# PSUM banks as tiles of their own, and a seven-product first MoE matmul with Silu for the last two batches

## The chip, the cores and the metric

The kernel runs on one core of a Trainium2 chip. The metric is the device time of one execution in microseconds (us). A core has engines that work side by side: TensorE (PE; its weight loads are PEld), VectorE (DVE), ScalarE (ACT), GpSimd (POOL) and SyncE (SP), which issues transfers. Matmul results land in PSUM, which the kernel uses as eight banks of 128 partitions by 512 fp32 values.

## The reference

Softmax attention for 8 batches, 12 heads, 448 tokens, head size 64. Its output, heads side by side, is the input of a two-layer block with a SiLU between (called MoE in the kernel):

```python
scores = q @ k.T / sqrt(64);  attn = softmax(scores);  y = attn @ v
x = y.transpose(0, 2, 1, 3).reshape(8 * 448, 768)
h = x @ w_in                       # 3584 x 768  times 768 x 2048
g = h * (1.0 / (1.0 + exp(-h)))    # SiLU
out = g @ w_out                    # 3584 x 2048 times 2048 x 768
```

## The kernel before

All matmul inputs are fp16, sums are fp32. A planner in Python (`Order`) walks a model of the engines and fixes the order in which each engine gets its instructions; the program then adds the waits that the data and the buffers need, by tile. The kernel is one core's, and every buffer is allocated once. These are its parts that the change and the prediction touch; cuts are marked with `# ...`.

PSUM and its banks. Banks 0 to 3 are for attention scores, in two pairs (a pair takes two heads); banks 4 to 7 (`M`) are for everything else: attention outputs, first and second MoE matmul. `lent()` says which score banks the rest may use when scores don't need them.

```python
P_s = [ps.tile([128, 2, 512], FP32, name=f"p_{i}") for i in range(4)]

def bank(i):
    return P_s[i // 2][:, i % 2]
# ...
M = (4, 5, 6, 7)

def lent():
    if not qk_seq or silu_phase() or LEND and e_slots.when(1) is None:
        return 0, 1, 2, 3
    return ()

def m_take():
    more = lent()
    i = min((*M, *more), key=lambda i: (banks.free[i] > od.now, i < 4, banks.free[i]))
    # ...
```

Attention (L383 scores, L408 Exp, L432 sums of Exp and products with V, L454/L459 inverse sums by transposes, L465 scaling):

```python
def expo(n, w, y, s_pair, e_i):
    # ...
    nc.scalar.activation(out=E_s[e_i][0:kr, 2 * y : 2 * y + 2, 0:nk],
                         in_=P_s[s_pair][0:kr, :, 0:nk], func=AF.Exp, scale=attn_scale)
# attend(): nc.tensor.matmul(out=bank(a)[32 * h : 32 * (h + 1), 0:nq], ...)      L432
# inverse(): nc.vector.transpose(out=t, in_=grouped(n, bank(a)))                 L454
# norm():    x = bank(a) * 0.5 * t   on VectorE, to x_s (xT in the profile)      L465
```

The first MoE matmul, plain form (all eight batches before the change). One of 16 blocks `f` of the hidden layer takes six matmuls into one bank. x carries a factor 0.5, so SiLU is (tanh(x) + 1) * x: a Tanh on ScalarE, then a gate on VectorE that reads the bank and writes G (or X):

```python
def ffn1_plain(b, f, t0, t1, a, c0, c1):
    for cc in range(c0, c1):
        nc.tensor.matmul(out=bank(a)[:, 0 : t1 - t0],                            # L485
            lhsT=w_in_t[:, cc, 128 * f : 128 * (f + 1)],
            rhs=x_s[x_at[(b, cc // HC)]][:, cc % HC, t0:t1], start=(cc == 0), # ...
def tanh(src, th):
    nc.scalar.activation(out=th, in_=src, func=AF.Tanh)                          # L498
def gate(eng, out, th, x):
    (nc.vector if eng == "DVE" else nc.gpsimd).scalar_tensor_tensor(             # L501
        out=out, in0=th, scalar=1.0, in1=x, op0=ALU.add, op1=ALU.mult)
def silu(out, src):
    nc.scalar.activation(out=out, in_=src, func=AF.Silu, scale=2.0)
# class Plain.run(), after the sixth matmul:
    done = od.add(Op("ACT", act(t1 - t0), lambda: tanh(x, th), [op], ...))
    # then, for each part, gate("DVE", dst[:, f, ...], th, x) with deps [done]; its end frees the bank
```

The first MoE matmul, folded form (class `Fold`), which is in the kernel before but used by no batch there. A batch's tokens, the 768 inputs and the 2048 hidden values are each halved, and a block of two by two halves is made from seven products (Strassen's scheme in Winograd's form) where the plain form takes eight. Each product is three matmuls of 224 columns; eight folds (`HF`) make a batch. Products 1, 2 and 5, 6, 3 share a bank side by side, 7 and 4 take a second bank:

```python
class Fold:
    ORDER = (1, 5, 2, 6, 7, 3, 4)
    # deps of product 1: the x of the batch, t_op (four differences of x on VectorE),
    #   and all output items that still read the part of G that this batch overwrites
    def run(self):
        # ... three matmuls of S // 2 = 224 columns
        if m == 5:   # copy products 1 and 5 (448 columns) on ScalarE or VectorE
        elif m == 6: # y = A + p1 on VectorE;  p5 = y - p5 on GpSimd
        elif m == 3: # c12 = A + p1 on VectorE, in the bank;  finish(bank, f)
        elif m == 4: # c21 = p5 + B on VectorE;  finish(F, f + HF)
        # after 6 and 7: c22 = B + y on VectorE
    def finish(self, src, ff, deps, psum):
        if b < SILU:   # Tanh, then gate, as in the plain form
        # else: Silu on ScalarE from src straight to G
```

While a batch with Silu is under way (`silu_phase()`), no new scores are started. The differences of `w_in` that folds need (`SI`, and one written over a quarter of `w_in`) are made in the kernel before as well.

The second MoE matmul (class `Quad`, L804): pairs of 128 tokens, 14 items in all, each also seven products, of eight matmuls of 384 columns, given to TensorE two at a time (`CUT = 2`). It works in two banks, `w` (products 1, 2, 3) and `q` (5, 6, 7, 4). Between products VectorE adds (L510) and ScalarE copies (L514) out of a bank; its left-hand sums (S, sometimes kept in E buffers) are added by VectorE and GpSimd from G.

```python
self.ORDER = (1, 5, 2, 6, 7, 3, 4)
# ... in run(): op = Op("PE", (i1 - i0) * mm(n), lambda: self.emit(m, a, ...))
if m == 1:   ev["p1"] = od.add(Op("ANY", {...}, lambda e: copy(e, p, W), [op], SLOW))
elif m == 5: add("r", r, Q, p, [op, ev["p1"]])
elif m == 2: ev["c11"] = self.write(0, 0, W, self.w, [op], None)
elif m == 6: add("y", W, Q, r, [op, ev["c11"]])
elif m == 7: add("c22", r, Q, r, [op, ev["y"]])   # ... and its store
elif m == 3: self.write(0, 1, W, self.w, [op], ...)
else:        add("c21", p, Q, p, [op, ev["c22"]], ...)   # ... and its store
```

Of the kernel before, what the change touches and what calls it, by code (L numbers as in the profile page):

```python
# [8 lines left out]
FP32 = mybir.dt.float32  # L9
# [191 lines left out]
def kernel(  # L201
# [28 lines left out]
    NT = 2 * S // 128  # L230
    OH = DM // 2
    PACE = 2.3
    DEFER, DITEM = .3, .1
    SUMS, EKEEP, ESENG = (0, 1), 2, 'VP'
    QB = 4
    LIM_H = 3
    LIM_E, LIM_S, LEND = 2, 2, 1
    LONE = NG + 1
    PLAIN = 8
    SILU = 8  # L240
    HIGH = 'POOL'
    ZENG = 'POOL'
    PIECES = ((0, 7), (7, TPP))
# [7 lines left out]
    ps = ctx.enter_context(tc.tile_pool(name="ps", bufs=1, space=bass.MemoryType.PSUM))  # L251
# [24 lines left out]
    x_s = [const.tile([128, HC, S], FP16, name=f"xT_{i}") for i in range(NX)]  # L276
    t_s = [const.tile([128, S], FP32, name=f"t_{i}") for i in range(NTMP)]
    S_s = [const.tile([128, HF, 128], FP16, name=f"S_{i}") for i in range(NSG)]
    P_s = [ps.tile([128, 2, 512], FP32, name=f"p_{i}") for i in range(4)]

    def bank(i):
        return P_s[i // 2][:, i % 2]


    units = []
# [130 lines left out]
    def attend(n, part, a, es, sums):  # L416
        b, hg, g0, g1 = units[n]
        nq = 32 * (g1 - g0)
        what = form(b, hg)
        chunks = [c for c in range(NCH) if part or c not in sums]  # L420
        if part == 0 and sums:
            chunks = [sums[0]] + chunks
        for c in chunks:
            rest = c == NCH - 1 and what != "lone"
            at = nq * (c % per_burst(n))
            kr = rows_of(n, c)
            for h in range(HG):
                if part == 0:
                    w = ones[0:kr, ("low", "high").index(what) + 1 if rest else 0]
                else:  # L430
                    w = V[0:kr, HG * hg + h, c, 32 * (part - 1) : 32 * part]
                nc.tensor.matmul(  # L432
                    out=bank(a)[32 * h : 32 * (h + 1), 0:nq],
                    lhsT=w,
                    rhs=E_s[sum_at[n] if part == 0 and c in sums else es[c // per_burst(n)]][
                        0:kr, h, at : at + nq
                    ],
                    start=(c == chunks[0]),
                    stop=(c == chunks[-1]),
                    skip_group_check=True,  # L440
                )
# [8 lines left out]
    def inverse(n, step, a, ti):  # L450
        g0, g1 = units[n][2:]
        t = grouped(n, t_s[ti])
        if step == 0:
            nc.vector.transpose(out=t, in_=grouped(n, bank(a)))  # L454
        elif step == 1:
            inv_t[n] = sb.tile([128, g1 - g0, 1], FP32, name=f"inv_{n}", tag="inv", bufs=2)
            nc.vector.reciprocal(out=inv_t[n], in_=t[:, :, 0:1])
        else:
            nc.vector.transpose(out=t, in_=inv_t[n].to_broadcast([128, g1 - g0, 32]))  # L459

    def norm(n, part, a, ti, xi):
        b, hg, g0, g1 = units[n]
        nq = 32 * (g1 - g0)
        cc = 2 * hg + part - 1
        nc.vector.scalar_tensor_tensor(  # L465
            out=x_s[xi][:, cc % HC, 32 * g0 : 32 * g1],
            in0=bank(a)[:, 0:nq],
            scalar=0.5,
            in1=t_s[ti][:, 0:nq],
            op0=ALU.mult,  # L470
            op1=ALU.mult,
        )


    def g_parts(b, t0, t1):
        cut = 6 * 128 - S if b % 4 == 1 else S
        r = b % 2
        for lo, hi, dst, at in ((0, cut, G, S * r), (cut, S, X, -cut)):
            lo, hi = max(lo, t0), min(hi, t1)
            if lo < hi:  # L480
                yield lo - t0, hi - t0, dst, at + lo
# [179 lines left out]
    def plan_turns(upto):  # L661

        while turned["n"] < min(upto, NU):
            if not plan_turn(turned["n"]):
                return
            turned["n"] += 1
# [49 lines left out]
    def plan_w_in_sums():  # L716
        for f in range(HF):
# [8 lines left out]
            def used(f=f):  # L726
                made = []
                for b in range(PLAIN):
                    got = plain_ops.get((b, f + HF), [])
# [132 lines left out]
    class Fold:  # L862
# [36 lines left out]
        def room(self):  # L899
            m = self.step()  # L900
            if m == 1:
                at = [x for x in (f_slots.when(1), e_slots.when(1)) if x is not None]
                return [min(at) if at else None]
            if m in (3, 4) and self.b < SILU:
                return [th_slots.when(1)]
# [23 lines left out]
        def run(self):  # L929
            m, n, ev = self.step(), S // 2, self.ev  # L930
            self.at += 1
            if m == 1:
                self.borrow = not f_slots.can(1, od.now)
                self.fi = (e_slots if self.borrow else f_slots).take(od.now)
                if self.b >= SILU and self.b not in silu_left:
                    silu_left[self.b] = NFF * len(list(g_parts(self.b, 0, S)))
# [43 lines left out]
        def finish(self, src, ff, deps, psum):  # L980
# [8 lines left out]

            if b < SILU:  # L990
                ti = th_slots.take(od.now)
# [43 lines left out]
    def plan_t(b):  # L1035

        if b in t_op or not all((b, c, 0) in x_op for c in range(NDC)):
            return
        if not T_slots.can(1, od.now):
            return  # L1040
        T_slots.take(od.now)
        n = S // 2
        x = {
            (h, t): x_s[x_at[(b, h)]][:, :, n * t : n * (t + 1)] for h in range(2) for t in range(2)
        }
        ops = [[x_op[(b, c, 0)] for c in range(HC * h, HC * (h + 1))] for h in range(2)]

        def sums(out, u, w, deps):
            return od.add(
                Op("DVE", half(HC * n), lambda: tt(out, u, w, ALU.subtract), deps, SLOW + 2)  # L1050
            )

        o1 = sums(T_s[:, 0], x[0, 1], x[0, 0], ops[0])
        o2 = sums(T_s[:, 1], x[1, 1], T_s[:, 0], [o1] + ops[1])
        o4 = sums(T_s[:, 2], x[1, 0], T_s[:, 1], [o2])
        o3 = sums(x[0, 1], x[1, 1], x[0, 1], [o1] + ops[1])
        t_op[b] = {1: o1, 2: o2, 3: o3, 4: o4}
# [14 lines left out]
    def s_place():  # L1072
        if s_slots.can(1, od.now):
            return "S", s_slots.take(od.now)
        if not qk_seq and not av_seq and len(t_op) == B - PLAIN and e_slots.can(1, od.now):
            return "E", e_slots.take(od.now)
# [185 lines left out]
    for b in range(B):  # L1262
        if b >= PLAIN:
            moe += [Fold(b, f) for f in range(HF)]
# [118 lines left out]

    def lent():
        if not qk_seq or silu_phase() or LEND and e_slots.when(1) is None:
            return 0, 1, 2, 3
        return ()

    silu_left = {}
# [1 line left out]
    def silu_phase():  # L1391
        return any(n > QB for n in silu_left.values())
# [4 lines left out]
    def m_when(n):  # L1397
        more = lent()
        at = sorted(banks.free[i] for i in (*M, *more))[n - 1]
        return None if at == NEVER else at  # L1400
# [4 lines that stand above are left out]
        assert banks.free[i] <= od.now  # L1405
        banks.free[i] = NEVER
        return i
# [184 lines left out]
    while True:  # L1592
        plan_turns(qk_seq[0][0][0] + 3 if qk_seq else NU)
        for b in range(PLAIN, B):
            plan_t(b)
# [73 lines left out]
```

## Time and profile before

| What | Value |
|---|---|
| Time, median of 3 runs | 525.39 us (523.48 to 526.75) |
| Span of the profiled execution | 523.3 us, 9760 instructions |
| PE (matmul) busy | 428.2 us, 82% |
| DVE busy | 281.6 us, 54% |
| ACT busy | 235.6 us, 45% |
| POOL busy | 210.6 us, 40% |
| Mean granted TensorE clock | 0.983 |
| First MoE matmul (L485), busy | 164.3 us, 864 matmuls |
| Second MoE matmul (L804, all forms), busy | 149.5 us |

A profile names instructions by engine, line of the kernel, operation, tile written and tiles read. "Busy" counts the time in which an instruction of the engine ran; matmuls are pipelined, so the end of a burst is counted too. "Idle before" is the time for which the engine stood still ahead of an instruction, and the name after the arrow is the instruction whose end released it. All PSUM tiles of this kernel share the name p in the profile, with the numbers left out, so that which bank is meant has to be found from the order of the instructions.

### The profile page before, as it was taken

Reading aid. Unit: us, or ns where it says so; the run is one execution under the profiler, and the core shown is the slowest. Engines: PE = TensorE matmul, PEld = TensorE weight load, DVE = VectorE, ACT = ScalarE, POOL = GpSimd, SP = SyncE. Lnnn points to the kernel's source line nnn. Section 1 sums busy time; section 2 is a strip of 40 time slices with the busy share of each in tenths; the row PEclk is TensorE's granted clock in tenths of the full one; section 3 lists DMA queues with packets and bytes.
Section 4 is the critical chain, followed back from the end, with each engine's and each line's share of the span. In section 5 each row is a group of like instructions: output and inputs, shape, how many; then the busy total and the mean of one; then the engine's idle time right before and its main releaser. Section 6 shows DMA issues by size and latency. Waiting matters only on the chain.

```text
span 523.3 us, 9760 instructions
## 1 busy us (share of the span) xinstructions
PE 428.2 (82%) x3853; PEld 210.9 (40%) x3853; DVE 281.6 (54%) x565; ACT 235.6 (45%) x356; POOL 210.6 (40%) x277
## 2 busy tenths in 40 slices
PE   8997787977589879888788987798788777779775
PEld 7655443332244334333333433343333433444332
DVE  2455866768756644663357534665466234624721
ACT  3876567767016564554236643457341123114210
POOL 5667969758542510851019510453033000302500
PEclk9999989999699999999999999999999999999989
DMA  8898065997043630653107520073000210021022
GB/s 117 113 183 135 2 85 77 186 169 112 1 76 85 92 75 1 77 97 79 31 1 98 105 75 5 8 115 63 3 1 22 58 41 1 16 76 31 0 54 69
DMA packets 38750, 34.46 MB, mean 66 GB/s; under 512 B 11952, under 2 KB 37936, under 8 KB 38704
## 3 DMA queue, kind: packets, MB, share of 16 engines
q0 software_dynamic: 27952, 22.82, 31.4%
q1 hardware_dynamic: 9984, 10.24, 7.2%
q10 hardware_dynamic: 768, 0.79, 0.6%
q8 instruction: 30, 0.49, 0.4%
q14 instruction: 16, 0.13, 0.1%
HBM read 45.61 MB, written 11.01 MB: 108 GB/s over the span
## 4 chain that ended last, share of the span: by engine, by line
PE 53%; DVE 17%; DMA 10%; ACT 8%; issue 7%; POOL 4%; DVEq 0%; ACTq 0%; POOLq 0%
PE p L485 22%; PE p L804 21%; PE p L432 7%; ACT th L498 6%; DMA rq<-in_q_dram 5%; DVE G L501 4%; PE p L383 3%; DMA w_in_t<-in_moe_w_in_dram 2%; DVE xT L465 2%; DVE t L510 2%; DVE S L510 2%; DVE E L510 2%; DMA rk<-in_k_dram 2%; DVE t L454 2%; POOL V L329 2%
## 5 line engine op out<-in xcount | busy, mean ns | idle before, releaser
L485 PE MATMUL p<-xT,w_in_t 128*128 128x448 f16 (+1 forms) x864 | 164.3, 333 | 37.3 <-ACT th L498 18.1
L408 ACT ACTIVATE E<-p 128x896 f16<-128x896 f32 (+1 forms) x172 | 148.6, 916 | 73.1 <-PE p L383 72.2
L501 DVE SCALAR_TENSOR_TENSOR G<-th,p 128x448 f16<-128x448 f16 (+2 forms) x144 | 76.3, 535 | 104.1 <-ACT th L498 47.7
L485 PEld LDWEIGHTS <-w_in_t 128*128 128x128 f16 x864 | 82.4, 98 | 117.8 <-issue 61.0
L498 ACT ACTIVATE th<-p 128x448 f16<-128x448 f32 (+1 forms) x144 | 70.5, 502 | 109.1 <-PE p L485 47.2
L804 PE MATMUL p<-w_out_t,G 128*128 128x384 f16 x304 | 61.4, 333 | 14.1 <-DVE t L510 6.8
L510 POOL TENSOR_TENSOR G<-G 128x512 f16<-128x512 f16 x21 | 25.1, 1206 | 95.5 <-DVE S L510 95.0
L514 ACT COPY t<-p 128x384 f32<-128x384 f32 x39 | 18.5, 478 | 99.6 <-PE p L804 79.4
L804 PEld LDWEIGHTS <-G 128*128 128x128 f16 x416 | 39.2, 99 | 57.1 <-issue 35.2
L383 PE MATMUL p<-QT,KT 32*128 32x448 f16 (+4 forms) x864 | 55.9, 342 | 2.3 <-ACT E L408 2.2
L329 POOL DMA_DIRECT2D V<-in_v_dram x88 | 48.9, 563 | 14.8 <-PE p L432 11.2
L432 PE MATMUL p<-E,V 128*32 128x448 f16 (+2 forms) x864 | 44.5, 337 | 8.0 <-DVE X L501 6.0
L804 PE MATMUL p<-TO,S 128*128 128x384 f16 x192 | 40.9, 340 | 12.1 <-DVE t L454 4.3
L510 DVE TENSOR_TENSOR t<-p,t 128x384 f32<-128x384 f32 x42 | 23.3, 554 | 49.4 <-PE p L804 46.4
L510 POOL TENSOR_TENSOR E<-E,E 128x896 f16<-128x896 f16 x18 | 35.5, 1971 | 31.9 <-ACT E L408 31.7
L804 PEld LDWEIGHTS <-S 128*128 128x128 f16 x280 | 26.0, 99 | 44.5 <-issue 29.2
L465 DVE SCALAR_TENSOR_TENSOR xT<-p,t 128x448 f16<-128x448 f32 (+1 forms) x54 | 30.2, 566 | 18.3 <-PE p L432 15.1
L432 PEld LDWEIGHTS <-V 128*32 128x32 f16 (+1 forms) x864 | 20.4, 96 | 28.8 <-issue 18.3
L510 POOL TENSOR_TENSOR G<-X,G 128x512 f16<-128x512 f16 x4 | 4.9, 1214 | 62.4 <-DVE S L510 62.4
L383 PEld LDWEIGHTS <-KT 32*128 32x128 f16 (+2 forms) x864 | 17.3, 98 | 29.9 <-issue 28.3
L454 DVE STREAM_TRANSPOSE t<-p 128x448 f32<-128x448 f32 (+1 forms) x27 | 16.0, 594 | 20.7 <-PE p L432 10.5
L804 PE MATMUL p<-TO,G 128*128 128x384 f16 x112 | 21.8, 326 | 4.3 <-ACT t L514 3.5
(60 smaller groups left out, 347.3 us busy)
## 6 DMA issues: line engine op xcount, KB each, us to landing
out_dram<-t SPq DMA_DIRECT2D x208, 48.0 KB, 1.6
rk<-in_k_dram POOLq DMA_DIRECT2D x24, 224.0 KB, 4.7
rq<-in_q_dram POOLq DMA_DIRECT2D x21, 224.0 KB, 5.2
w_out_t<-in_moe_w_out_dram POOLq DMA_DIRECT2D x8, 384.0 KB, 7.8
V<-in_v_dram POOLq DMA_DIRECT2D x43, 64.0 KB, 2.8
V<-in_v_dram POOLq DMA_DIRECT2D x40, 48.0 KB, 2.5
w_in_t<-in_moe_w_in_dram POOLq DMA_DIRECT2D x16, 96.0 KB, 4.6
w_in_t<-in_moe_w_in_dram POOLq DMA_DIRECT2D x8, 192.0 KB, 8.4
```

The source lines that it names most:

```text
L329: nc.gpsimd.dma_start(out=V[32 * x : 32 * (x + 1), hs, 0:count, :], in_=v[b, hs].rearrange("h (i g) d -> i h g d", g=TPP)[:, :, first : fi ...
L383: nc.tensor.matmul(out=P_s[s_pair][p0 : p0 + 32 * (x1 - x0), h % 2, at : at + nq], lhsT=KT[(b, hg)][32 * h : 32 * (h + 1), c, x0:x1, :, e] ...
L408: nc.scalar.activation(out=E_s[e_i][0:kr, 2 * y : 2 * y + 2, 0:nk], in_=P_s[s_pair][0:kr, :, 0:nk], func=AF.Exp, scale=attn_scale,)
L432: nc.tensor.matmul(out=bank(a)[32 * h : 32 * (h + 1), 0:nq], lhsT=w, rhs=E_s[sum_at[n] if part == 0 and c in sums else es[c // per_burst(n)]][
L454: nc.vector.transpose(out=t, in_=grouped(n, bank(a)))
L465: nc.vector.scalar_tensor_tensor(out=x_s[xi][:, cc % HC, 32 * g0 : 32 * g1], in0=bank(a)[:, 0:nq], scalar=0.5, in1=t_s[ti][:, 0:nq], op0=A ...
L485: nc.tensor.matmul(out=bank(a)[:, 0 : t1 - t0], lhsT=w_in_t[:, cc, 128 * f : 128 * (f + 1)], rhs=x_s[x_at[(b, cc // HC)]][:, cc % HC, t0:t ...
L498: nc.scalar.activation(out=th, in_=src, func=AF.Tanh)
L501: (nc.vector if eng == "DVE" else nc.gpsimd).scalar_tensor_tensor(out=out, in0=th, scalar=1.0, in1=x, op0=ALU.add, op1=ALU.mult)
L510: e.tensor_tensor(out=out, in0=a, in1=b, op=op)
L514: nc.scalar.copy(out=out, in_=in_)
L804: nc.tensor.matmul(out=bank(a)[:, 0 : self.n], lhsT=lhs(i), rhs=rhs(i), start=(start and i == 0), stop=(i == last), skip_group_check=True,)
```

## The change

Two things are done together. First, the banks 4 to 7 become four tiles of one bank each (names p), and only the two score pairs stay tiles of two banks (names s), so that the program's waits on banks 4 to 7 go by the bank. As halves of a pair are still one tile, only one bank of each score pair is lent. Second, batches 6 and 7 use the folded form of the first MoE matmul, with seven products for eight, and Silu on ScalarE for Tanh and gate; that takes work from TensorE, and the gates from VectorE. A constant of the planner, the time for which TensorE is held free ahead of scores that are about to be ready, is halved.

```diff
-    DEFER, DITEM = .3, .1
+    DEFER, DITEM = .15, .1
 ...
-    PLAIN = 8
-    SILU = 8
+    PLAIN = 6
+    SILU = 6
 ...
-    P_s = [ps.tile([128, 2, 512], FP32, name=f"p_{i}") for i in range(4)]
+    P_s = [ps.tile([128, 2, 512], FP32, name=f"s_{i}") for i in range(2)]
+    B_s = [ps.tile([128, 512], FP32, name=f"p_{i}") for i in range(4)]
 
     def bank(i):
-        return P_s[i // 2][:, i % 2]
+        return P_s[i // 2][:, 0] if i < 4 else B_s[i - 4]
 ...
     def lent():
         if not qk_seq or silu_phase() or LEND and e_slots.when(1) is None:
-            return 0, 1, 2, 3
+            return 0, 2
         return ()
```

## The prediction

> **What bounds the kernel now.** I read the table of stretches first, split where the work changes: loading and the first two batches, then attention mixed with MoE, then MoE alone (the last Exp starts before 400 us). Columns: length, then busy us and instruction count of PE, weight loads, DVE, ACT and POOL, the granted clock, DMA share and GB/s.
>
> ```profile
> 0.00:140.00 140.00, 112.64 (x1463) 63.30 (x1464) 88.50 (x201) 87.18 (x131) 101.54 (x143) 0.96 0.75 110
> 140.00:400.00 260.00, 220.72 (x1872) 98.78 (x1874) 144.55 (x283) 123.40 (x177) 90.51 (x117) 0.99 0.33 55
> 400.00:523.30 123.30, 94.86 (x524) 48.80 (x524) 48.53 (x84) 25.03 (x48) 18.51 (x17) 0.98 0.15 38
> ```
>
> TensorE is the busiest engine everywhere, yet 95 us of the span it is idle, and after 140 us nothing else comes near its own limit: DVE is at 56% and 39%, ACT at 47% and 20%, DMA at 0.33 and 0.15. So after 140 us the time is lost between engines. Next the waits of TensorE, longest in total first (us, times, longest):
>
> ```profile
> PE p L485 <- ACT th L498: 18.1, 27, 1.0
> PE p L804 <- DVE t L510: 13.8, 16, 2.2
> PE p L485 <- DVE G L501: 10.6, 19, 2.7
> PE p L804 <- ACT t L514: 6.7, 12, 0.6
> PE p L432 <- DVE X L501: 6.0, 2, 5.8
> ```
>
> All these releasers read PSUM; only 1.2 us in the whole list is a DMA. The first line is odd: a bank of the plain MoE matmul is free when the gate (L501) has read it, and the gate comes after the Tanh (L498). A matmul released by a Tanh waits for a Tanh on some other bank. The timeline of batch 6's plain products (420 to 443 us) shows the pattern, here one period of 3.12 us (start, duration, engine, idle before and releaser):
>
> ```profile
> 432.11 2.43 PE L485 MATMUL p<-xT,w_in_t 128*128 128x448 f16 x12 [0.69 <-ACT th L498]
> ...
> 433.14 0.62 DVE L501 SCALAR_TENSOR_TENSOR G<-th,p 128x448 f16<-128x448 f16 x1 [1.27 <-PE p L485]
> 433.79 0.54 ACT L498 ACTIVATE th<-p 128x448 f16<-128x448 f32 x1 [1.73 <-DVE G L501]
> 434.44 0.62 DVE L501 SCALAR_TENSOR_TENSOR G<-th,p 128x448 f16<-128x448 f16 x1 [0.68 <-ACT th L498]
> 434.64 0.54 ACT L498 ACTIVATE th<-p 128x448 f16<-128x448 f32 x1 [0.30 <-PE p L485]
> 435.24 2.05 PE L485 MATMUL p<-xT,w_in_t 128*128 128x448 f16 x10 [0.69 <-ACT th L498]
> ```
>
> Twelve matmuls fill two banks. A Tanh waits until a gate has ended (433.14 + 0.62 = 433.76, Tanh at 433.79), and a gate waits for TensorE, though each Tanh and gate has its own bank. In the code banks 4 and 5 are halves of one tile, so are 6 and 7: the program takes a hold on one half for a hold on both. I therefore read these as false waits. The tail has the same thing in the other MoE matmul, where a product in one bank waits after two matmuls for the evacuation of the last product's bank:
>
> ```profile
> 504.50 0.56 DVE L510 TENSOR_TENSOR t<-p,t 128x384 f32<-128x384 f32 x1 [3.32 <-PE p L804]
> ...
> 505.12 1.14 PE L804 MATMUL p<-w_out_t,S 128*128 128x384 f16 x6 [0.65 <-DVE t L510]
> 506.09 0.49 PE L804 MATMUL p<-TO,G 128*128 128x384 f16 x2
> ...
> 506.61 0.48 ACT L514 COPY t<-p 128x384 f32<-128x384 f32 x1 [4.31 <-DMA out_dram<-t]
> ...
> 507.14 1.14 PE L804 MATMUL p<-TO,G 128*128 128x384 f16 x6 [0.57 <-ACT t L514]
> ```
>
> **What the Trainium skill says.** "PSUM — Partial Sum Buffer", section "PSUM bank collisions raise a hardware error": two engines must be kept off one bank and quadrant at once, reads included, while different banks run clean. That makes a wait per bank necessary and a wait per pair of banks needless; this trace shows only the needless kind working, and the separation of banks itself no run has shown yet. "Perfetto Trace Analysis", section "Matmuls": independent groups should rotate through banks so that evacuation overlaps the next group. The planner rotates, and the trace shows that it does not overlap. "TensorE: Matmul & The Clock Gate", section "Back-to-back issue gap": N/2.4 + 2.5 ns. The trace agrees: bursts of 12, 8 and 4 matmuls of 448 columns take 2.43, 1.68 and 0.92 us, so 0.189 each plus 0.16 for the end of a burst; 8, 4 and 2 of 224 columns in the first batch take 0.93, 0.56 and 0.35, so 0.097; 8 and 2 of 384 take 1.46 and 0.49, so 0.162. "ScalarE: Activation LUTs", section "What ACT_TABLE_LOAD costs": 1283 ns for the load alone. The one load here took 1283.
>
> **The change, part one: tiles of one bank.** It adds no instruction. It removes waits. I sum by stage, and with each removed wait the 0.16 us of a burst's end goes too, since the next matmul follows at once.
>
> MoE alone, 400 to 523. Streaming work: 300 matmuls of 384 columns x 0.162 = 48.6, 192 of 448 x 0.189 = 36.3, 32 of attention (16 take 0.94, 12 take 0.75, so 0.0475 each) = 1.5; together 86.4 of 123.3, so 36.9 us are no streaming. Of these 3.9 are the last add and store after the last matmul (519.4 to 523.3), about 2 a lowered clock near 499 us (six matmuls in 1.98 instead of 1.14, and the neighbours), about 5 waits for the S sums of the second matmul (2.25 at 494.6, 1.79 at 451, 0.43, 0.4), which are true data. I leave 3 for switches. So about 14 stay and some 22 can go.
>
> Attention and MoE, 140 to 400. Waits sum to 38.7 us in about 60 places: L485 <- Tanh 13.3, L485 <- gate 4.5, L804 <- attention's readers (L454, L465) 8.9, L804 <- its own adds and copies (L510, L514, L516) 9.0. The period above falls from 3.12 to 12 x 0.189 = 2.27 if DVE (2 x 0.62) and ACT (2 x 0.54) keep up, which they do. I take four fifths of the first two (14) and two thirds of the others (12), the rest being true uses of a bank, and 45 ends of bursts x 0.16 = 7. Sum 33.
>
> Loading, 0 to 140: 26.4 us of waits, but DMA at 0.75 and POOL at 101 of 140 us busy; transfers and their buffers set this stage. I take a third: 8.
>
> Lending: attention's score banks are lent to MoE only as two (0 and 2) instead of four, so six banks at the end instead of eight. A plain product needs one and an output item two, with two items open, so I put nothing on this. The smaller hold before scores (0.15 for 0.3) reorders TensorE in the middle stage; I give it nothing either.
>
> **Part two: seven products for eight in batches 6 and 7.** TensorE: before 96 matmuls x 0.189 = 18.1 us a batch; after 8 folds x 21 matmuls of 224 columns x 0.097 = 16.3. Minus 1.8 a batch, 3.7 in all. ACT: 16 Tanh of 0.54 = 8.7 a batch become 16 Silu of the same length and, if it takes them, 8 copies of 448 columns at about 0.53, sum 13, and one table load of 1.28 for the run of Silu. DVE: 16 gates x 0.62 = 9.9 become 8 x 4 adds of 224 columns. There is no row for these; 448 and 224 columns of the gate take 620 and 378, so 1.08 ns a column, and 384 columns of an add take 554, hence 0.38: sum 12.2, and four differences of x of 672 elements, about 2. DVE then holds 14 of 16.3 us: close. POOL: one subtraction a fold, about 0.6. The chain of a fold (product, copy, product, add, subtraction, add, Silu) is some 4.5 us, and three folds are open for 2.04 us of TensorE each, so it is just covered. The sums of w_in (SI) are made in the kernel before as well and cost nothing new. I expect 0 to 4 us of gain, 2.
>
> **Sum.** 22 + 33 + 8 + 2 = 65. Of such a sum some is taken up by new, true limits, as DVE works in order and would be 65% busy; I keep nine tenths, 59. **525.4 - 59 = 466 us.**
>
> **The rivals.** (a) The waits are true and only change their name: the freed matmul then waits for the gate of its own bank, or DVE is late. For it: DVE's in-order queue at 494 to 496 us, where additions of 1.37 us delay the add that TensorE waits for. Against it: DVE at 39 to 56%, a Tanh released by a gate of another bank. It would make some 500. (b) The fold costs more than it gives: DVE is at its limit, the second batch's folds must wait for all older outputs, fewer banks are lent. For it: 14 of 16.3 us. It would add 5 to 10: 473. (c) Loading paces more than the first stage: the chain of waits holds 10% DMA and 4% POOL, with transfers of 4 to 6 us at 171, 182 and 220 us. A faster TensorE would meet them sooner; the middle stage then gives half, 483. (d) Everything overlaps: efficiency of streaming above 90% after 140 us, 448.
>
> **Range and chances.** (b) and (c) are each likely enough to be partly true, (d) sets the low end, (a) wholly is unlikely. So 449 to 487. To miss 2% the false waits would have to give under 11 us, while Tanh and gate alone hold TensorE for 17.8 between 140 and 400 us: faster 0.94, same 0.04, slower 0.02.
>
> **What would show it.** Right: L485 <- Tanh gone from TensorE's waits; in plain batches bursts that run on, 2.27 us per two banks; tail waits of 0.57 and 0.65 gone; TensorE idle near 50 us, DVE over 60%; folds of about 2.1 us each, one more table load. Wrong: TensorE's waits keep their sum under DVE's name (a); a fold phase of over 18 us a batch, with waits on DVE's adds (b); waits of L432 or L383 on DMA or transposes grown (c). What I trust least is the middle stage's 33 us.

## The result, and the profile after

The changed kernel takes **444.05 us** (443.31 to 447.0) against 525.39: a ratio of 0.847 (95% interval 0.840 to 0.854), 81 us less. The prediction was 466 us with a range of 449 to 487. The direction and the mechanism hold; the time lies below the range, so the size has to be explained.

Lines of the kernel have moved by one (L485 is now L486, L804 now L805; L921 is the fold's matmul). Score tiles are now called s, the others p. First the stretches, with borders that are the same instructions in both kernels: the first burst of 16 score matmuls of shape 32*64 after the sums of w_out (155.60 us before, 144.18 after) and the end of the last attention product (401.56 and 347.80). Columns as in the first table of the prediction; the kernel before:

```profile
0.00:155.60 155.60, 126.23 (x1533) 70.44 (x1533) 98.72 (x223) 88.52 (x134) 108.41 (x153) 0.96 0.70 104
155.60:401.56 245.96, 208.69 (x1832) 92.34 (x1831) 135.68 (x263) 122.06 (x174) 84.35 (x109) 1.00 0.32 55
401.56:523.30 121.74, 93.30 (x496) 48.11 (x492) 47.19 (x80) 25.03 (x48) 17.80 (x17) 0.98 0.15 38
```

and the changed kernel:

```profile
0.00:144.18 144.18, 127.11 (x1531) 69.66 (x1531) 101.14 (x225) 87.98 (x132) 107.87 (x152) 0.91 0.73 109
144.18:347.80 203.62, 199.75 (x1832) 92.44 (x1832) 140.41 (x273) 120.32 (x173) 87.53 (x114) 1.00 0.40 70
347.80:441.50 93.70, 82.56 (x634) 60.97 (x634) 53.99 (x116) 32.91 (x64) 24.15 (x27) 1.00 0.20 50
```

The stages give 11.4, 42.3 and 28.0 us. In the middle, TensorE is busy for 199.75 of 203.62 us with the same 1832 matmuls: it hardly stands still any more, and DVE (140 of 204) is not the bound. The waits of TensorE, longest first:

```profile
PE p L433 <- DVE X L502: 7.6, 1, 7.6
PE p L486 <- DVE G L502: 3.6, 1, 3.6
PE p L805 <- DVE t L511: 3.1, 3, 1.6
PE p L805 <- DVE S L511: 2.6, 2, 1.4
```

The Tanh that stood first (18.1 us in 27 places) is gone from the list, the output item's adds went from 13.8 to 3.1. What stands first now is one single wait, at 121 us. As the prediction asked of a right account, TensorE is idle for 32 us in all (near 50 was put), DVE is busy for 67% of the span, a fold takes 2.0 us, and there is one more table load. Batch 5's plain products, by the timeline, run as one burst:

```profile
319.75 13.79 PE L486 MATMUL p<-xT,w_in_t 128*128 128x448 f16 x72
```

72 x 0.189 + 0.16 = 13.77: twelve matmuls take 2.27 us, as worked out, for 3.12 before (batch 6; batch 5 had 3.1 to 3.2). The chain that ended last is now 76% PE (53% before), 12% DVE (17%) and 5% DMA (10%).

### The profile page after: what moved, and what is told of

It reads as the page before. It is cut to its first block, busy times and chain, and to the rows that moved or that the text cites. A ratio compares the mean times of both kernels' runs of the same rounds, so it can differ in the third digit from the quotient of the medians.

```text
span 441.5 us, 10112 instructions
## 1 busy us (share of the span) xinstructions
PE 409.4 (93%) x3994; PEld 223.1 (51%) x3994; DVE 295.5 (67%) x612; ACT 241.2 (55%) x369; POOL 219.5 (50%) x292
## 4 chain that ended last, share of the span: by engine, by line
PE 76%; DVE 12%; DMA 5%; issue 3%; POOL 3%; SPq 0%; ACT 0%; DVEq 0%; ACTq 0%; POOLq 0%
PE p L486 25%; PE p L805 25%; PE p L433 11%; PE s L384 8%; PE p L921 6%; DVE E L511 3%; DMA rk<-in_k_dram 2%; DVE S L511 2%; DMA rq<-in_q_dram 2%; PE s L921 1%; POOL w_in_t L340 1%; DVE SI L511 1%; DVE xT L466 1%; POOL V L330 1%; DMA w_in_t<-in_moe_w_in_dram 1%
## 5 line engine op out<-in xcount | busy, mean ns | idle before, releaser
L409 ACT ACTIVATE E<-s 128x896 f16<-128x896 f32 (+1 forms) x172 | 148.9, 915 | 66.1 <-PE s L384 65.4
L486 PE MATMUL p<-xT,w_in_t 128*128 128x448 f16 (+1 forms) x672 | 120.7, 332 | 6.1 <-DVE G L502 3.6
L486 PEld LDWEIGHTS <-w_in_t 128*128 128x128 f16 x672 | 63.7, 100 | 61.5 <-issue 19.7
L502 DVE SCALAR_TENSOR_TENSOR G<-th,p 128x448 f16<-128x448 f16 (+2 forms) x112 | 56.1, 510 | 38.4 <-ACT th L499 37.8
L499 ACT ACTIVATE th<-p 128x448 f16<-128x448 f32 (+1 forms) x112 | 53.2, 495 | 44.0 <-PE p L486 41.5
L805 PE MATMUL p<-w_out_t,G 128*128 128x384 f16 x304 | 59.2, 330 | 2.2 <-DVE p L511 1.5
L384 PE MATMUL s<-QT,KT 32*128 32x448 f16 (+4 forms) x864 | 58.5, 346 | 1.3 <-ACT E L409 1.0
L805 PEld LDWEIGHTS <-G 128*128 128x128 f16 x416 | 38.6, 98 | 37.2 <-issue 14.2
L511 POOL TENSOR_TENSOR G<-G 128x512 f16<-128x512 f16 x23 | 27.7, 1210 | 59.2 <-DVE S L511 57.5
L805 PE MATMUL p<-TO,S 128*128 128x384 f16 x192 | 38.5, 335 | 5.7 <-DVE t L511 3.1
L805 PEld LDWEIGHTS <-S 128*128 128x128 f16 x288 | 26.3, 99 | 32.6 <-issue 13.5
L466 DVE SCALAR_TENSOR_TENSOR xT<-p,t 128x448 f16<-128x448 f32 (+1 forms) x53 | 29.6, 563 | 14.0 <-PE p L433 12.9
L363 DVE STREAM_TRANSPOSE KT<-rk 128x256 f32<-128x256 f32 (+3 forms) x48 | 16.6, 384 | 16.9 <-DMA rk<-in_k_dram 16.9
L805 PE MATMUL p<-TO,G 128*128 128x384 f16 x112 | 21.2, 326 | 0.0
```

Of the source, the lines that this page charges most:

```text
L384: nc.tensor.matmul(out=P_s[s_pair][p0 : p0 + 32 * (x1 - x0), h % 2, at : at + nq], lhsT=KT[(b, hg)][32 * h : 32 * (h + 1), c, x0:x1, :, e] ...
L466: nc.vector.scalar_tensor_tensor(out=x_s[xi][:, cc % HC, 32 * g0 : 32 * g1], in0=bank(a)[:, 0:nq], scalar=0.5, in1=t_s[ti][:, 0:nq], op0=A ...
L486: nc.tensor.matmul(out=bank(a)[:, 0 : t1 - t0], lhsT=w_in_t[:, cc, 128 * f : 128 * (f + 1)], rhs=x_s[x_at[(b, cc // HC)]][:, cc % HC, t0:t ...
L511: e.tensor_tensor(out=out, in0=a, in1=b, op=op)
L805: nc.tensor.matmul(out=bank(a)[:, 0 : self.n], lhsT=lhs(i), rhs=rhs(i), start=(start and i == 0), stop=(i == last), skip_group_check=True,)
```

## Experiments

The change bundles three things, so the first question is which one brought the surplus over the prediction: false waits that were more numerous than I allowed (A), my allowance being right for the waits (B), or the changed order of instructions, which the hold and the lending alter (C). Times are compared with runs of the kernel before beside them (527.7, 526.5 and 525.7 us in the three groups).

### Tiles of their own and nothing else: own_banks

```diff
-    P_s = [ps.tile([128, 2, 512], ...) for i in range(4)]
+    P_s = [ps.tile([128, 2, 512], ...) for i in range(2)]; B_s = [ps.tile([128, 512], ...) for i in range(4)]
-        return P_s[i // 2][:, i % 2]
+        return P_s[i // 2][:, i % 2] if i < 4 else B_s[i - 4]
```

> The kernel before with banks 4 to 7 as tiles of their own and nothing else: the order of instructions on every engine is that of the kernel before, the four score banks stay lent. Theory A (nearly all waits of TensorE on readers of PSUM were false; I kept too many as true): about 450 us, the middle stage (end of the TO stall to the last attention product) near 220 us. Theory B (my prediction: a third of the middle's waits are true and a tenth is lost again): about 468 us, middle near 235. Theory C (the surplus comes from the changed order of instructions, not from the waits): about 470 us, and the 25 us more appear only with the new hold. Rival (a), waits only change their name: about 500 us or more.

Measured: **443.6 us**, ratio 0.843 (0.837 to 0.849). That is all of the change's gain, with every engine given the same instructions in the same order as before (3853 matmuls on TensorE in both). B and C fall. Between the two borders it takes 202.64 us (142.90 to 345.54) for 245.96. One period of plain products in its timeline:

```profile
361.80 4.51 PE L485 MATMUL p<-xT,w_in_t 128*128 128x448 f16 x23
...
362.57 0.54 ACT L498 ACTIVATE th<-p 128x448 f16<-128x448 f32 x1 [0.59 <-PE p L485]
363.15 0.62 DVE L501 SCALAR_TENSOR_TENSOR G<-th,p 128x448 f16<-128x448 f16 x1 [0.52 <-ACT th L498]
```

Here the Tanh waits for TensorE alone and the gate for its Tanh alone; TensorE runs on. Over the whole span, ScalarE's idle time ahead of a Tanh that a gate released fell from 37.9 us in 22 places to 0.6 in one. All waits of TensorE fell from 89.0 us in 128 places to 26.7 in 21; between the two borders from 36.7 us in 57 places to 2.1 in 4.

### One pair shared, one separate: half_own

```diff
-    P_s = [ps.tile([128, 2, 512], ...) for i in range(4)]
+    P_s = [ps.tile([128, 2, 512], ...) for i in range(3)]; B_s = [ps.tile([128, 512], ...) for i in range(2)]
+        return P_s[i // 2][:, i % 2] if i < 6 else B_s[i - 6]
```

> As the run with own banks, but banks 4 and 5 remain halves of one tile; 6 and 7 get their own. Order of instructions unchanged. If the cost is the sharing of a tile (A), every second pair still stalls: between the two, 480 to 500 us, the stall of 0.69 us after every second pair of products of the plain first MoE matmul. If bank count or order mattered and not sharing, the same as one of the two ends.

Measured: 491.5 us, 0.934 (0.929 to 0.940), waits of 61.4 us in 84 places. The shared pair is called p in its timeline, as are the score pairs; the separate banks are b:

```profile
395.57 2.43 PE L485 MATMUL b<-xT,w_in_t 128*128 128x448 f16 x12
...
397.84 1.68 PE L485 MATMUL p<-xT,w_in_t 128*128 128x448 f16 x8
...
400.15 0.92 PE L485 MATMUL p<-xT,w_in_t 128*128 128x448 f16 x4 [0.63 <-ACT th L498]
400.90 2.43 PE L485 MATMUL b<-xT,w_in_t 128*128 128x448 f16 x12
...
401.17 0.62 DVE L501 SCALAR_TENSOR_TENSOR G<-th,p 128x448 f16<-128x448 f16 x1 [1.94 <-PE p L485]
```

Twelve matmuls into the separate banks pass without a stop; those into the pair stop in the middle, and the pair's gate waits for TensorE to leave its neighbour. Of the waits, 55.6 us in 79 places are of matmuls into p, 5.8 us in 5 places of matmuls into b. The wait sits where the sharing is.

### All four banks one tile: one_tile

```diff
-    P_s = [ps.tile([128, 2, 512], ...) for i in range(4)]
+    P_s = [ps.tile([128, 2, 512], ...) for i in range(2)]; B_s = ps.tile([128, 4, 512], ...)
-        return P_s[i // 2][:, i % 2]
+        return P_s[i // 2][:, i % 2] if i < 4 else B_s[:, i - 4]
```

> The opposite: banks 4 to 7 are one tile of four banks, order of instructions unchanged. If waits go by the tile, a plain product then waits for Tanh and gate of the product just before: per product about 6 x 0.189 + 0.16 + 0.54 + 0.62 and handoffs, 2.6 us instead of 1.56, so over 7 batches of 16 about 110 us more, with the second MoE matmul's share 620 to 680 us in all. If waits go by the bank within a tile, 525 us as before.

Measured: 840 us, far beyond the expectation, in the same order of instructions again. A second execution took 856 us at a lower clock and is left aside, so there is no interval. The span of 838.1 us is 314.8 longer than before. Waits are 264.4 us in 387 places, 175 more; the other 139 are in PE's busy time (567.6 for 428.2). The expectation counted a burst's end but kept its matmuls at full speed, and here they were not:

```profile
602.74 0.54 ACT L498 ACTIVATE th<-p 128x448 f16<-128x448 f32 x1 [3.68 <-DVE X L501]
603.33 1.65 PE L485 MATMUL p<-xT,w_in_t 128*128 128x448 f16 x4 [1.01 <-ACT th L498]
```

Four matmuls take 1.65 us, 0.37 each and an end: half speed, and the granted clock from 599 to 608 us is 0.50. Its mean in four stretches of the run is 0.73 to 0.85, with a stop of 0.7 us on the mean every 2.2 us. That the stops lower the clock is not shown by itself: the kernel before, with 128 stops of the same mean length, one every 4.1 us, ran at 0.983. The time follows the number of banks in a tile: 444, 491, 528 and 840 us for one, a mixture, two and four; the waits of TensorE are 27, 61, 89 and 264 us.

### Without the fold: no_fold

```diff
-    PLAIN = 6
-    SILU = 6
+    PLAIN = 8
+    SILU = 8
```

> The changed kernel with all eight batches in the plain form and with Tanh (no fold, no Silu); own tiles, two banks lent, the new hold of 0.15. Fold worth what I predicted (2 us): 446 us. Fold worth its TensorE work plus its tail (4 to 6): 448 to 450. If the fold brought much of the surplus: 455 to 465.

Measured: 446.0 us, 0.849 (0.840 to 0.857), against 0.847 for the whole change: no difference outside the intervals.

### The lending, the fold and the hold one by one: after_again, tiles_lend2, defer_old

after_again is the changed kernel. defer_old takes back its hold (`DEFER = .3`), tiles_lend2 takes back hold and fold, so that its order of instructions is that of the kernel before.

> The changed kernel once more, as the anchor for the other kernels of this chip: 442 to 446 us, 0.845 of before.

> Own tiles, two score banks lent for four, old hold, no fold; the order of instructions is that of the kernel before. If lending four banks is worth something, slower than the run with own banks (443.6) by some us; my prediction put nothing on it: 443 to 445.

> The changed kernel with the old hold of 0.3: own tiles, two banks lent, fold and Silu in batches 6 and 7. Against the run with two banks lent it shows the fold alone. Fold worth its TensorE work: 3.7 us less, 440. Fold's savings lost in its end (last adds and Silu before the output items, sums of G late): the same within 1 us. Against the changed kernel it shows the new hold: nothing by my prediction; a gain or loss of over 2 us would be the order of instructions.

Measured: after_again 445.9 us, 0.846 (0.843 to 0.849); tiles_lend2 442.7, 0.8405 (0.837 to 0.844); defer_old 442.8, 0.8404 (0.837 to 0.843). Lending two banks for four costs nothing that these intervals would show (own_banks has 0.843); the fold nets nothing here; the shorter hold, if anything, loses some 3 us (the intervals just touch; no_fold against tiles_lend2, which also differ in the hold alone, points the same way with 0.849 against 0.8405). Where the fold's gain goes, the MoE-only stretch tells, first without the fold (tiles_lend2), from the end of the last attention product:

```profile
347.73:442.20 94.47, 85.83 (x493) 47.88 (x492) 47.45 (x80) 25.04 (x48) 17.73 (x17) 0.99 0.19 49
```

and with it (defer_old):

```profile
349.23:443.10 93.87, 82.89 (x637) 61.18 (x636) 53.83 (x115) 32.85 (x64) 24.13 (x27) 1.00 0.20 49
```

TensorE is busy for 2.9 us less, but the stretch shrinks by 0.6 only: waits rise from 4.8 to 7.0 us, those on the S sums alone from 0.6 to 2.6: the output items wait longer for their sums. Fold and Silu were taken in and out together in every run, so what each of them does alone is not shown.

### The fold on shared tiles: fold_only

```diff
-    PLAIN = 8
-    SILU = 8
+    PLAIN = 6
+    SILU = 6
```

> The kernel before with fold and Silu in batches 6 and 7 and nothing else: shared tiles. Each fold makes four more evacuations than a plain pair and works in two banks of shared tiles, so every product of three short matmuls may stall on the neighbour: plain batches 3.12 and 2.58 us a pair become 3.5 to 4.5 us a fold, so 530 to 545 us. If the fold were good by itself: 520 to 523.

Measured: 525.1 us, 0.998 (0.996 to 1.001): neither the loss expected nor a gain. From 401.56 us on its waits sum to 23.9 us (24.2 before), of which the folds' own matmuls (L920 there) have 8.9 in 20 places. The expectation was wrong in the number of stops more than in their length: about half a us each, but 20 in the 112 products of 16 folds.

### The longest wait left: late_w_out, w_on_dve, w_on_dve_plain, adds_on_dve

own_banks has its longest wait, 6.98 us, at nearly the same place as the changed kernel its 7.6. The kernel before had it as well, a stop of 5.76 us that makes up most of the fifth line of the prediction's list of waits. First the matmul that follows the stop, in the kernel before and in own_banks:

```profile
135.00 1.68 PE L432 MATMUL p<-E,V 128*32 128x448 f16 x16 [5.76 <-DVE X L501]
```

```profile
131.62 4.36 PE L804 MATMUL p<-TO,S 128*128 128x384 f16 x16 [6.98 <-DVE S L510]
```

The timeline of own_banks there, DVE and POOL:

```profile
118.85 0.55 DVE L510 TENSOR_TENSOR w_out_t<-w_out_t 128x768 f16<-128x768 f16 x1
...
122.11 1.63 POOL L510 TENSOR_TENSOR TO<-w_out_t,TO 128x768 f16<-128x768 f16 x1
122.47 8.29 DVE L510 TENSOR_TENSOR w_out_t<-w_out_t 128x768 f16<-128x768 f16 x1
...
123.71 1.86 POOL L510 TENSOR_TENSOR E<-E,E 128x896 f16<-128x896 f16 x1
...
128.72 1.62 POOL L510 TENSOR_TENSOR TO<-w_out_t,TO 128x768 f16<-128x768 f16 x1
```

An add that takes VectorE 0.55 us at 118.85, while GpSimd does none, takes 8.29 while GpSimd streams five adds without a gap, and ends 0.4 us after the last of them. In the kernel before, the four sums of w_out that VectorE does ahead of the stop took 1.4 to 2.0 us each beside GpSimd's adds; in own_banks, with none beside them, the same four took 0.5 to 0.55. The Trainium skill, "SBUF — State Buffer", section "Who interferes with whom", says that a VectorE instruction with two SBUF inputs contends with GpSimd instructions that read SBUF; the trace agrees, and shows the delay lasting over five of them.

late_w_out only lowers the priority of these sums (`TB = 30` for 5 in the changed kernel):

> The changed kernel with the differences of w_out (TO) given the lowest priority in the planner (30 for 5), so that VectorE takes gates and attention first. Theory: the longest wait left, 7.6 us at 121 us with a lowered TensorE clock after it, is VectorE's queue with four of these additions of 1.7 to 3 us each ahead of two gates. If so the wait shrinks and 4 to 8 us are gained: 436 to 440. If the output items need the differences at that very time, the wait moves to the second MoE matmul and nothing is gained: 443 to 446.

Measured: 442.9 us, 0.8405 (0.838 to 0.843), for the changed kernel's 0.8458: about 3 us, with intervals that just touch. The wait shrank to 4.9 and one add of 3.23 us remained in front of the gates. Less than expected; GpSimd still had its part of the sums.

w_on_dve starts from defer_old and gives all sums of the weights to VectorE; w_on_dve_plain does so from tiles_lend2:

```diff
-    WENG = 'VP'
+    WENG = 'DVE'
```

> Own tiles, two banks lent, fold and Silu, old hold (442.8 before), and the sums of both weight matrices (SI, TO) on VectorE alone, none on GpSimd. Theory: the longest wait left (7 to 10 us at 122 us) is a VectorE add of two SBUF inputs that cannot run while GpSimd streams adds of its own without a gap (7.93 us for an add that takes 0.55 otherwise). Then the wait goes and the lowered TensorE clock after it too: 432 to 437. Rival: VectorE simply has too much ahead of the gates there; with the whole of the weight sums on VectorE (16 TO adds x 0.55 = 9 us instead of half) it gets no better or worse: 442 to 447.

> The run with the weight sums on VectorE, without fold and Silu (all batches plain, Tanh). If fold is worth nothing net, as at the old place of these sums: equal to that run within 1 us. If the fold's 3 us of TensorE come through once the other waits are shorter: 2 to 3 us slower than that run.

Measured: 436.8 us, 0.829 (0.825 to 0.833), and 438.9 us, 0.834 (0.830 to 0.838). The wait of 7 to 10 us is gone (the longest left are 2.5 and 2.9); 6 and 4 us are gained, where some 6 to 11 were expected of the first. The rival, no better or worse, falls. The fold now looks worth 2 us, within the intervals.

adds_on_dve takes the Exp and S sums from GpSimd as well:

```diff
-    SUMS, EKEEP, ESENG = (0, 1), 2, 'VP'
+    SUMS, EKEEP, ESENG = (0, 1), 2, 'DVE'
-    VPS = (3, 4)
+    VPS = ()
```

> As the run with the weight sums on VectorE, and the sums of Exp and of G (S) on VectorE too; GpSimd keeps one subtraction a fold. If GpSimd's adds cost VectorE more than they take off it (adds of 1.37 us where 0.41 is usual): 2 to 6 us less than that run. If VectorE becomes the bound of the middle stage (75 to 80% busy): 440 to 450.

Measured: **424.7 us**, 0.806 (0.802 to 0.811), some 20 us under the changed kernel, 12 under w_on_dve where 2 to 6 were expected, and the best here. The groups of w_on_dve show what these adds cost (count | busy us, mean ns):

```profile
L511 POOL TENSOR_TENSOR E<-E,E 128x896 f16<-128x896 f16 x20 | 38.1, 1905 | 36.6 <-ACT E L409 36.4
L511 DVE TENSOR_TENSOR E<-E,E 128x896 f16<-128x896 f16 x18 | 22.2, 1236 | 1.4 <-ACT E L409 1.4
```

beside those of adds_on_dve:

```profile
L511 DVE TENSOR_TENSOR E<-E,E 128x896 f16<-128x896 f16 x36 | 21.5, 614 | 0.9 <-ACT E L409 0.9
```

Alone, VectorE does 36 Exp sums in less time (21.5 us) than 18 beside GpSimd (22.2). Its whole busy time falls from 296.7 to 285.6 us although it took GpSimd's adds over. Waits of TensorE are down from 21.4 to 12.2 us. How much of the 12 us comes from VectorE being undisturbed, and how much from sums that are ready sooner (614 ns for GpSimd's 1905), no run separates.

## Why the prediction was right and where it failed

**What bounds the kernel**: right. The time was lost between engines, and the releaser that belongs to another bank was the mark of it. own_banks shows it with nothing else changed, half_own and one_tile show that the loss follows the sharing.

**The step that failed** is how much of each stage's waits was taken as removable: a third while loading, four fifths and two thirds in the middle, 22 us in MoE alone, and a tenth off the sum. The mechanism was right; the tiles alone took 83.3 us off the span (523.3 to 440.0) where 63 less a tenth had been put. The first stage has the largest part of it. Its border at 140 us is taken at one matmul that has the same 1465 matmuls ahead of it in both kernels, first in the kernel before, then in own_banks:

```profile
0.00:140.82 140.82, 113.46 (x1465) 63.61 (x1466) 88.71 (x201) 87.18 (x131) 101.54 (x143) 0.96 0.74 110
```

```profile
0.00:123.18 123.18, 109.97 (x1465) 62.99 (x1466) 80.62 (x199) 86.43 (x131) 93.11 (x139) 0.96 0.83 125
```

**Loading, 8 us**: 17.6, so here the prediction was furthest off. I let DMA and GpSimd set this stage and took a third of its 26.4 us of waits; 12.9 are left, with a DMA share of 0.83 for 0.74. Of the difference 5.8 us is the stop behind VectorE's slow adds, which only moved: it lies ahead of this border before and behind it with own banks. Up to the later border (155.60 and 142.90), behind the stop in both, 12.7 us remain, still more than 8.

**The middle stage, 33 us**: 38.5 from this border (260.74 to 222.29), or 43.3 from the later one (245.96 to 202.64). I kept a fifth of the waits on Tanh and gate and a third of the others as true uses of a bank. From the later border 34.6 of 36.7 us went, 94%, and with 53 ends of bursts x 0.16 = 8.5 that makes 43.1. The view that would have said so was at hand: with four banks in turn and six matmuls (1.14 us) to a bank, a bank's reader has over 3 us before the bank is needed, and Tanh and gate take 1.2.

**MoE alone, 22 us** (its own terms, 36.9 less 13.9, give 23.0): the tiles alone took 27.3 here (121.74 to 94.46). Waits fell by 19.4 us, and 34 places x 0.16 is 5.4. The half-speed clock near 499 us, which I had kept, did not come (0.99 for 0.98): some 1.5 us more, from six matmuls in 1.98 us instead of 1.14 and twice two in 0.84 instead of 0.49. About 1 us stays open, and of the 3 us kept for switches nothing shows. The waits that I took as true stayed: 1.79, 0.43 and 2.25 us before, 1.94, 0.57 and 1.59 with own banks.

**The tenth taken off for new limits, 6 us**: wrong. No engine became the bound, DVE at 65% had room. The longest stop left, 6.98 us, is no new limit either; it was 5.76 before.

**The fold, 2 us**: measured 0 to 2, never outside the intervals. Its adds took 0.38 to 0.40 us and the copy 0.53, as worked out, and TensorE was full in the folds (13.0 of 13.0 us from 361 to 374); in the one pair of profiles compared, the gain went into waits for the later S sums. **Lending**: nothing, as put. **The hold**: put at nothing, perhaps a loss of 3 us.

**The rivals**: (a), waits that change their name, fell with own_banks. (b), a fold that costs 5 to 10 us, fell as well; within the intervals it neither costs nor pays. (c), loading that paces the middle, fell: 203.62 us with a DMA share of 0.40. (d), streaming at over 90%, was put at 448 as the low end and is what happened, with TensorE busy for 95% of the time after 144 us and 444 us in all; the range rested on (b) and (c) being partly true.

## What to carry to other kernels

Where a wait's releaser works on another bank than the instruction that waits, look at what the program counts as one buffer before looking for a faster engine; make each unit that is filled and emptied by itself a tile of its own. And when such waits are found to be false, count them whole, in every stage, with the end of each broken burst: a share kept as true needs a reason from the trace. Adds of two SBUF inputs on a helper engine are not free for VectorE; look at the mean of the same group alone and beside it.

## What the runs showed of the hardware that was not expected

- A VectorE add of 0.55 us lasted 8.29 us beside a stream of five GpSimd adds (own_banks). Giving VectorE all of GpSimd's adds but the folds' subtraction lowered VectorE's own busy time by 11.7 us (297.3 in defer_old, 285.6 in adds_on_dve).
- In one_tile, with 387 stops of 0.7 us on the mean, the mean granted TensorE clock was 0.78 over the whole run, so that the list of waits told little more than half of the loss: 175 us of waits came with 139 us of slower matmuls and burst ends.
- After the single stop of 6.98 us in own_banks the next 16 matmuls of 384 columns took 4.36 us instead of 16 x 0.162 + 0.16 = 2.75; the mean granted clock was 1.00 from 124.7 to 128.0 us and 0.50 from 128.1 to 134.8, so it fell during the stop.
